# Sliding-window attention into a two-layer MLP: 96-row query and key loads, 544-column key blocks, a reordered opening and attention steps ahead of each group

## The chip, the cores and the metric

One core of one Trainium2 chip. The metric is device time in microseconds (us) of one execution, as the median of several. Engines are named TensorE (PE in the profile, PEld for its weight loads), VectorE (DVE), ScalarE (ACT), GpSimd (POOL) and SyncE (SP, which here only issues transfers).

## The reference

```python
# q, k, v: (8 batches, 8 heads, 576 tokens, 64), float32
scores = scale * q @ k^T;  masked to |i - j| <= 32;  softmax over j
x = (attn @ v) as (4608 tokens, 512)
h = x @ w_in            # (512, 2048)
g = max(0.01 * h, h)
out = g @ w_out         # (2048, 512)
```

The two products of the MLP are 589,824 of the 737,280 columns that TensorE streams in the kernel before. The attention is small for TensorE, but each of its 64 steps (a batch, half of its tokens, a pair of heads) passes through all four engines.

## The kernel before

A step scores the next pair and finishes the present one. `weighted` is the part that VectorE paces: one `s` buffer and one `x` buffer, a reciprocal (1.96 us in the profile before), a multiply (0.46 us).

```python
def score(i):            # five matmuls into ps, exp on ScalarE, mask multiply on GpSimd -> pr
    ...
def weighted(i):         # ones_bd x pr -> s (row sums), vbd x pr -> x
    ...
    nc.vector.reciprocal(r, s)
    nc.vector.tensor_mul(xT[:, p, t0:t0 + HALF], x, r)

def step():
    i = state["done"]; b, r = i // 8, i % 8
    step_transposes(...)             # next batch's q and k, a group at a time
    if i + 1 < NC: score(i + 1)
    weighted(i)
    if r in (0, 1): cast_qk(b + 1, r)          # GpSimd
    if r == 2: load_qks(b + 2)
    if 2 <= r < 6: cast_v(b + 1, r - 2)        # GpSimd
    if r == 6: load_vs(b + 2)
    state["done"] += 1
```

The queries and keys come in with 64 tokens of a head on 64 partitions, in pieces of 256 bytes. The MLP takes the tokens in groups of 256, then 512; each group is cut into chunks (a few h tiles, or one o tile), and a group's share of attention steps is spread over its chunks, each step BEHIND its chunk:

```python
groups = [(0, 256)] + [(256 + 512 * i, 512) for i in range(8)] + [(256 + 512 * 8, 256)]
need = [4 * -(-(t0 + n) // HALF) for t0, n in groups]   # steps that a group's tokens need
...
for ci, (kind, a, m) in enumerate(chunks):
    want = start + -(-(goal - start) * (ci + 1) // len(chunks))
    todo = want - state["done"]
    ...                                # the chunk's h tiles or its o tile
    for _ in range(todo):
        step()
```

The softmax here doesn't subtract the row's maximum and nothing guards it: scores larger than these inputs give would overflow.

## Time and profile before

| | before |
|---|---|
| median of the runs | 421.28 us (418.67 to 422.35) |
| profiled span | 421.2 us |
| mean granted TensorE clock | 0.974 |

The page's first part gives busy us, share of the span and instructions of each engine; in its second part each digit is the busy share (or granted clock) of a fortieth of the span, 10.5 us, in tenths.

```profile
PE 338.7 (80%) x2464; PEld 194.5 (46%) x2464; DVE 202.3 (48%) x204; ACT 164.5 (39%) x289; POOL 176.5 (42%) x220
...
PEclk9999999989999899989999999999899989989999
DMA  9999999445871937192450956396301100110111
```

The DMA engines are full (busy 90% or more) for the first seven slices. The clock dips six times, one slice each, to 0.8.

### The profile page before, as it was taken

The page shows a single profiled execution, that of the slowest core. Times are in us where ns is not written, and L with a number is a line of the kernel's source. Part 1 is how long each engine was busy: PE and PEld are TensorE (multiplying, and loading weights), DVE is VectorE, ACT ScalarE, POOL GpSimd, SP SyncE. Part 2 cuts the span into 40 slices and gives each one's busy share as a digit, 9 for nine tenths or more (in the row PEclk, how much of TensorE's full clock was granted, in tenths as well). Part 3 has the DMA queues.
Part 4 walks back from the last instruction along what each step waited for, and adds up shares of the span by engine and source line. Part 5 has one row for each costly group of instructions (what it writes and reads, how often), then busy time and mean ns, then how long its engine had stood idle before and what let it go on. Part 6 is the DMA issues. An engine that isn't in the chain of part 4 may idle for free.

```text
span 421.2 us, 6100 instructions
## 1 busy us (share of the span) xinstructions
PE 338.7 (80%) x2464; PEld 194.5 (46%) x2464; DVE 202.3 (48%) x204; ACT 164.5 (39%) x289; POOL 176.5 (42%) x220
## 2 busy tenths in 40 slices
PE   0231058766999799979999997999899799989996
PEld 0120046643555365545555554565455445534472
DVE  6112043866466457634445765568357735740111
ACT  1140033622752274237237525732473255116050
POOL 8992153746426443633216553654355413200000
PEclk9999999989999899989999999999899989989999
DMA  9999999445871937192450956396301100110111
GB/s 163 207 202 198 190 136 193 77 69 122 130 114 61 205 60 138 61 199 43 92 121 4 197 136 102 65 188 128 60 0 46 55 2 2 51 50 2 50 51 50
DMA packets 119835, 42.33 MB, mean 100 GB/s; under 512 B 112640, under 2 KB 114688, under 8 KB 119808
## 3 DMA queue, kind: packets, MB, share of 16 engines
q1 hardware_dynamic: 117056, 37.76, 50.7%
q0 software_dynamic: 2752, 4.20, 5.5%
q8 instruction: 19, 0.31, 0.3%
q14 instruction: 8, 0.07, 0.1%
HBM read 36.70 MB, written 9.44 MB: 110 GB/s over the span
## 4 chain that ended last, share of the span: by engine, by line
PE 73%; POOL 9%; DVE 7%; SPq 3%; issue 3%; ACT 3%; DMA 2%; POOLq 0%; DVEq 0%
PE mm L236 31%; PE mm L245 29%; DVE r L224 5%; PE s L217 3%; SPq L65 3%; PE tp L168 3%; PE x L217 3%; PE ps L197 3%; DMA kf<-in_k_dram 2%; POOL pr L205 2%; POOL mask L128 1%; POOL mask L124 1%; DVE xT L226 1%; ACT qT L174 1%; POOL w_in_bf L290 1%
## 5 line engine op out<-in xcount | busy, mean ns | idle before, releaser
L236 PE MATMUL mm<-xT,w_in_bf 128*128 128x512 bf16 (+1 forms) x640 | 142.3, 380 | 17.2 <-DVE xT L226 17.2
L224 DVE RECIPROCAL r<-s 128x288 f32<-128x288 f32 x64 | 125.2, 1957 | 58.0 <-PE s L217 56.6
L205 POOL TENSOR_TENSOR pr<-e,mask 128x576 bf16<-128x576 bf16 x64 | 81.4, 1272 | 169.2 <-ACT e L203 168.8
L245 PE MATMUL mm<-w_out_bf,gT 128*128 128x512 bf16 x576 | 130.7, 382 | 0.0
L240 ACT ACTIVATE gT<-mm 128x512 bf16<-128x512 f32 (+1 forms) x160 | 88.7, 554 | 94.0 <-PE mm L236 92.7
L236 PEld LDWEIGHTS <-w_in_bf 128*128 128x128 bf16 x640 | 64.0, 103 | 81.8 <-issue 30.0
L245 PEld LDWEIGHTS <-gT 128*128 128x128 bf16 x576 | 54.8, 99 | 62.1 <-issue 1.7
L250 DVE COPY o_sb<-mm 128x512 f32<-128x512 f32 x36 | 24.9, 691 | 70.8 <-PE mm L245 70.8
L174 ACT ACTIVATE qT<-tp 128x640 bf16<-128x640 bf16 (+1 forms) x32 | 20.7, 648 | 80.4 <-PE tp L168 80.4
L187 DVE COPY kbd<-tp 64x640 bf16<-64x640 bf16 (+1 forms) x32 | 14.8, 461 | 76.8 <-ACT kbd L185 76.7
L203 ACT ACTIVATE e<-ps 128x576 bf16<-128x576 f32 x64 | 41.2, 643 | 22.5 <-PE ps L197 22.4
L168 PE MATMUL tp<-ident,qb 128*128 128x128 bf16 x144 | 14.7, 235 | 35.7 <-POOL qb L147 31.9
L185 ACT ACTIVATE kbd<-tp 64x640 bf16<-64x640 bf16 (+1 forms) x32 | 20.5, 641 | 48.5 <-PE tp L168 48.5
L217 PE MATMUL s<-pr,ones_bd 128*128 128x128 bf16 (+1 forms) x320 | 27.7, 220 | 8.3 <-POOL pr L205 7.4
L226 DVE TENSOR_TENSOR xT<-x,r 128x288 bf16<-128x288 f32 x64 | 29.3, 458 | 6.7
L168 PEld LDWEIGHTS <-qb 128*128 128x128 bf16 x144 | 11.5, 105 | 42.0 <-POOL qb L147 32.3
L197 PE MATMUL ps<-qT,kbd 128*128 128x128 bf16 (+1 forms) x320 | 27.9, 220 | 1.2 <-ACT e L203 1.1
L217 PE MATMUL x<-pr,vbd 128*128 128x128 bf16 (+1 forms) x320 | 27.9, 220 | 0.1
L168 PE MATMUL tp<-ident,kb 128*128 128x128 bf16 x144 | 14.6, 234 | 16.0 <-ACT qT L174 8.3
L197 PEld LDWEIGHTS <-kbd 128*128 128x128 bf16 x320 | 22.6, 102 | 5.1 <-issue 2.3
L217 PEld LDWEIGHTS <-ones_bd 128*128 128x128 bf16 x320 | 20.0, 101 | 9.3 <-DVE r L224 5.0
L147 POOL CAST qb<-qf 128x1152 bf16<-128x1152 f32 x16 | 18.3, 1143 | 12.2 <-DMA qf<-in_q_dram 12.1
(25 smaller groups left out, 123.2 us busy)
## 6 DMA issues: line engine op xcount, KB each, us to landing
qf<-in_q_dram SPq DMA_DIRECT2D x32, 288.0 KB, 5.3
kf<-in_k_dram SPq DMA_DIRECT2D x32, 288.0 KB, 6.1
vf<-in_v_dram SPq DMA_DIRECT2D x16, 576.0 KB, 7.5
out_dram<-o_sb SPq DMA_DIRECT2D x36, 256.0 KB, 2.1
w_in_bf<-in_moe_w_in_dram POOLq DMA_DIRECT2D x8, 256.0 KB, 9.0
w_out_bf<-in_moe_w_out_dram POOLq DMA_DIRECT2D x4, 512.0 KB, 13.1
```

What stands on the lines that cost most here:

```text
L168: nc.tensor.transpose(tp[:, c - c0].rearrange("p s i -> p (s i)"), src[:, c, u].rearrange("p a d -> p (a d)"), ident,)
L174: nc.scalar.activation(out=qT[b][:, :, u, 64 * c0:64 * c1].rearrange("p s (c i) -> p c s i", i=64), in_=tp[:, 0:n], func=AF.Copy,)
L197: nc.tensor.matmul(ps[:, c0:c0 + n], kbd[b % 2][:, p, blk, :], qT[b][:, p // 2, p % 2, q0:q0 + n], start=True, stop=True,)
L203: nc.scalar.activation(out=e, in_=ps[:, 0:576], func=AF.Exp, scale=scale)
L205: nc.gpsimd.tensor_mul(pr, e, mask[hf])
L217: nc.tensor.matmul(dst[:, a:a + n], ones_bd if w is None else w[:, p, blk, :], pr[:, c0:c0 + n], start=(n_ == 0), stop=(n_ == len(WIN[hf]) ...
L224: nc.vector.reciprocal(r, s)
L226: nc.vector.tensor_mul(xT[:, p, t0:t0 + HALF], x, r)
L236: nc.tensor.matmul(h[:, 0:n], w_in_bf[:, c, ts(f, 128)], xT[:, c, ds(t0, n)], start=(c == 0), stop=(c == DMC - 1),)
L240: nc.scalar.activation(out=gT[g][:, f, 0:n], in_=h[:, 0:n], func=AF.Prelu, alpha=0.01)
L245: nc.tensor.matmul(o, gT[g][:, f, ts(j, 128)], w_out_bf[:, f, :], start=(f == 0), stop=(f == FFC - 1),)
L250: nc.vector.tensor_copy(out=o_sb, in_=o)
```

## The change

The intent: fewer, longer pieces in the loads; less to load before the first weights; no wait for xT at the start of a group. Its parts:

1. **Layout.** Each of 96 partitions holds six consecutive tokens (1536 bytes a piece). Transposes give the tokens in another order, put right while ScalarE and VectorE read PSUM. Key blocks are ordered so that 544 columns do for 576, and s takes two matmuls for five. The two masks are copied out of one window, which GpSimd builds with 4 select instructions in place of 40.
2. **Reordered opening.** Batch 0 goes pair by pair through cast, transpose, score and step; the weights are issued behind all four pairs; batch 1's loads are held behind the last weight by two tiny transfers; the h tiles of the first 512 tokens are computed before batch 1's attention begins. From here on the q and k loads of the batch after next stand behind a batch's seventh step, not its third.
3. **Attention ahead.** Steps are issued AHEAD of a chunk, by a rule that must have a group's steps done two chunks before the group starts.

```diff
-    t = fload.tile([128, 2, 2, NB, D], FP32, name=name)        # 64 rows, 256-byte pieces
+    qf[b] = fload.tile([96, NPAIR, 2, RUN * D], FP32, name="qf")  # RUN = 6 tokens a row
 ...
+                tok = tp.rearrange("p c i -> p i c")              # token order while PSUM is read
+                    nc.scalar.activation(out=qT[b][:, p].rearrange("p (i c) -> p i c", c=RUN), in_=tok, func=AF.Copy)
 ...
-        if r == 2:
-            load_qks(b + 2)
-        if r == 6:
-            load_vs(b + 2)
+            if r == 6 and b + 2 < B:
+                new_batch(b + 2); load_qk(b + 2, 0, 4); load_v(b + 2, 0, 4)
 ... opening
+    for p in range(NPAIR):
+        cast_qk(0, p, p + 1, nc.vector)
+        next(first); next(first)
+        cast_v(0, p)
+        if p == 0: score(0)
+        else: step()
+    for fq in range(4): load_w_in(512 * fq, 512 * fq + 512)
+    ...                                   # w_out; clears of kbd[1], vbd[1] on GpSimd
+    ...                                   # tiny transfers from w_out into qf[1], kf[1]; then batch 1's loads
+    step()
+    for f in range(FFC):
+        h_tile(0, 256, f)
+        if f % 4 == 3: step()
+    for f in range(FFC): h_tile(256, 256, f)
+    cast_qk(1, 0, 4); ...                 # casts of v
+    o_tile(0, 0); o_tile(0, 1)
+    step_transposes(16)
+    ...
 ... pacing
+    groups = [(512, 256)] + [(768 + 512 * i, 512) for i in range(7)] + [(768 + 512 * 7, 256)]
+    LEAD = 2
+    for ci, (_, kind, t0, n, a, m) in enumerate(chunks):
+        ahead = chunks[min(ci + LEAD, len(chunks) - 1)][0]
+        goal = max(ahead, base + -(-(NC - base) * (ci + 1) // span))
+        while state["done"] < min(goal, NC):
+            step()
+        ...                               # the chunk
```

## The prediction

> **What bounds the kernel now.** I read the page (shares, chain), then a table of stretches, then TensorE's waits, then the timeline of the opening and of one group of attention steps. TensorE is 80% busy and the chain is 73% TensorE, but the busy share hides two different halves. In the table of stretches (columns: stretch, length, busy time of PE, PEld, DVE, ACT, POOL, granted clock, DMA share, GB/s):
>
> ```profile
> 22.00:66.40 44.40, 12.48 (x104) 10.54 (x104) 11.77 (x13) 8.09 (x13) 22.39 (x28) 1.00 1.15 184
> ...
> 120.00:400.00 280.00, 261.92 (x1864) 142.35 (x1862) 148.34 (x150) 118.98 (x203) 108.17 (x108) 0.97 0.43 82
> ```
>
> Before 66 us TensorE is nearly idle while the DMA engines are full; after it TensorE sets the pace. The timeline shows what the opening waits for: the batch-1 key load, caught in a queue with all weights.
>
> ```profile
> 46.60 1.14 POOL L147 CAST qb<-qf 128x1152 bf16<-128x1152 f32 x1 [12.12 <-DMA qf<-in_q_dram]
> ...
> 54.94 1.15 POOL L147 CAST kb<-kf 128x1152 bf16<-128x1152 f32 x1 [7.20 <-DMA kf<-in_k_dram]
> ...
> 66.45 3.78 PE L236 MATMUL mm<-xT,w_in_bf 128*128 128x256 bf16 x17 [1.73 <-DVE xT L226]
> ```
>
> TensorE's waits from 66.4 us to the end, in us, times, longest:
>
> ```profile
> PE mm L236 <- DVE xT L226: 17.2, 8, 2.3
> PE tp L168 <- ACT qT L174: 5.4, 6, 1.0
> PE s L217 <- POOL pr L205: 2.9, 3, 1.0
> ```
>
> Each group of 512 tokens begins with an h tile that waits 2 us for the attention step just ahead of it: one reciprocal and one multiply on VectorE. The last thing to read is the pace of two attention steps with nothing between them:
>
> ```profile
> 79.97 0.42 PE L217 MATMUL s<-pr,ones_bd 128*128 128x128 bf16 x5
> ...
> 80.43 1.96 DVE L224 RECIPROCAL r<-s 128x288 f32<-128x288 f32 x1 [1.65 <-PE s L217]
> ...
> 82.58 0.41 PE L217 MATMUL s<-pr,ones_bd 128*128 128x128 bf16 x5 [1.00 <-POOL pr L205]
> ...
> 83.44 1.96 DVE L224 RECIPROCAL r<-s 128x288 f32<-128x288 f32 x1
> ```
>
> The s tile has one buffer, so the second step's s starts only after the first reciprocal: 2.6 us from s to s, of which TensorE works 0.95. A step that stands alone between two chunks of matmuls costs TensorE nothing extra; a step next to another costs it about 1.7 us.
>
> **Budget of now.** Sixteen 512-column matmuls start at 108.11 and the next instruction at 111.57: 3.46 us, 0.422 ns a column. All matmuls move 737,280 columns (589,824 in the two products, 3 x 64 x 576 attention, 288 x 128 transposes): 311 us. At 66.45 some 14,400 of these are done (6.1 us), so the opening loses 60.4. The last copy ends at 417.96 and the end is 421.2: with the copy, a tail of 3.9. The middle loses the rest, 46: waits of 28.5 (17.2 for xT), and half-speed clock windows of about 10 (granted clock 0.83 in 90 to 100 us, 0.96 in five of the seven 40 us stretches up to 400), 7 unnamed.
>
> [...] batch 0, loaded 64 partitions at a time, moves at 206 GB/s from 4 to 18 us. [...] the change takes q and k to 1536 bytes. [...]
>
> **The change part by part.**
> *Loads.* Packets of q and k fall from 73,728 to 12,288. After 90 us the DMA share is under two thirds and TensorE waits for a load-fed cast only once (2.7 us), so in the middle this is worth about 3 us. It counts in the opening alone.
> *544 columns.* 64 x 32 x 3 columns fewer: 731,136, or 308.5 us; minus 2.6. s takes 2 matmuls for 5. GpSimd's multiply falls from 1.27 to an estimated 1.20 us.
> *96-row transposes.* 384 x 96 columns, the same as now. ScalarE copies 576 columns twice a pair, about 0.65 us each as the 640/512 ones do (0.70/0.60); VectorE's two key copies replace one of 0.46 by two of perhaps 0.25. GpSimd casts 96 x 768 per pair, a third more elements: 64 x 0.77 against 32 x 1.145, plus 12 us, which the mask (11 us) pays. None of these is near a bound.
> *Opening.* GpSimd's order is the crux. It first clears vbd as 4608 elements (0.83 ns each from the two memset forms, 3.9 us), then builds the window, ready near 8 us. Then for each of four pairs: key cast 0.8, transposes 0.75, PSUM copy 0.75, two key copies 0.6, score 0.75, exp 0.65, multiply 1.3, and only then the next pair's key cast. That is 5.7 us a pair, so the weight loads, placed behind the fourth multiply, are issued near 34 us (19 now), with the DMA engines idle from about 18. Weights took 28 us from first issue (19.0) to the last landing (about 47); alone I keep 27: 61 us. Behind them GpSimd clears two more tiles (8 us), so the fifth multiply and with it the second h chunk start near 53; the h tiles of 512 tokens end near 73, two o tiles near 80. Batch 1 is loaded only after the weights: k lands near 75, v near 81, casts to 86. Eight transpose groups at 1.2 us run 80 to 89, the first score, exp and multiply bring steady work to 92 us. By then TensorE has done batch 0's attention, 16 transpose groups, 512 tokens of h and 256 of o: 72,500 columns, 30.6 us. The opening loses 61 us: as much as now.
> *Attention ahead.* The order of the changed kernel's TensorE queue shows the xT wait gone: o tiles of the last group stand between a group's last attention step and its first h tile. But the rule "be ahead two chunks before the group" makes steps come in bunches: two runs of six, three or so of three, some of two, and chunks of 64 matmuls with no step at all. I count 19 steps that stand right behind another (now 4 after the opening). 19 x 1.75 = 33 us; the runs of six also hold the next batch's q and k casts, 3.1 us of GpSimd per step for two steps: plus 5. Single-buffer transposes as now: 5. Clock windows at half speed after 7 to 8 such runs: 10. Together 53 against 46 now.
>
> Sum: 308.5 + 61 + 53 + 3.9 = 426.
>
> **Rivals.** (1) *The opening is much shorter*: if pairs pipeline at 4 us instead of 5.7 and the memsets are cheap, weights start near 25 us and steady work near 80: about 412, or 400 with the bunches milder than counted. For it: 15 us less of small-packet traffic ahead of the weights, and a plan that was clearly meant for this. Against it: GpSimd's multiply stands in its queue ahead of the next cast. (2) *The xT wait goes and the bunches are absorbed*: minus 17 and nothing back, about 390 to 400. Against it: one s buffer and 2.6 us a step, seen three times in the trace. (3) *The bunches cost more*: casts of a batch just loaded block GpSimd in the middle of a run, [...]the next chunk runs at half speed: 440. (4) *Strided PSUM reads slow ScalarE*: at double cost plus 40 us on an engine busy 164: it would stay below TensorE's total but lengthen every h chunk; about 435.
>
> **Range and chances.** The sum reproduces the kernel before only up to 7 us that I could not name, and the opening is a chain of some 25 links, each good to a tenth. That is 12 us either way around 426; against it, a reordering with such tuned constants was probably kept because it helped. I take 424, 399 to 441. Below 412.9 is faster by 2%: 0.28. Between: 0.38. Above 429.7: 0.34.
>
> **What would show it.** Right: weight loads issued after 30 us; a DMA gap in front of them; the first o tile after 70 us and steady work near 90; "s waits for reciprocal or multiply" as the largest wait of TensorE in the middle, 25 us or more, in two runs near the first two 512-token groups; no xT wait of note. Wrong: weights issued by 25 us; h tiles dense from 45 us; runs of six taking under 12 us; a middle (after steady work begins) losing under 35 us. ScalarE's copies at 1 us or more would be rival 4. What would make the total wrong most easily is the opening: every microsecond of the pair chain counts four times.

Its sum: 308.5 (columns) + 61 (opening) + 53 (middle) + 3.9 (tail) = 426. The 10 us of half-speed clock within the 53 are the author's estimate, carried over from the old trace (0.83 at 90 to 100 us, 0.96 in five later stretches).

## More of the kernel before

One more view is used later, the table of stretches for 31.3 us of the steady part, with the reciprocals (one for each attention step) that run in it, from the view of the r tile:

```profile
105.80:137.10 31.30, 30.51 (x246) 17.72 (x245) 19.20 (x19) 16.73 (x29) 15.12 (x15) 1.00 0.60 102
```

```profile
L224 DVE RECIPROCAL r<-s x7: 1947/1958/1958, 108.1 to 135.8; 128x288 f32<-128x288 f32 x7
```

TensorE is busy 30.5 of 31.3 us while seven steps pass. Where seven steps meet 30 us of matmul columns, they are hidden.

## The result, and the profile after

| | before | after |
|---|---|---|
| median of the runs of the same rounds | 420.45 us | 447.91 us (445.89 to 447.93) |
| ratio of fast runs | | 1.0641 [1.0581, 1.07] |
| profiled span | 421.2 us | 444.2 us |
| mean granted clock | 0.974 | 0.915 |

A ratio is the mean time of one kernel's fast runs over that of the other's fast runs of the same rounds, so it is not quite the ratio of the medians. Executions over 1.5% slower than the fastest of the same kernel are left out of the means. The result is correct and 6.4% slower, above the predicted range.

The page after, the lines that answer to those of before (a slice is now 11.1 us):

```profile
PE 351.4 (79%) x2432; PEld 201.8 (45%) x2432; DVE 220.6 (50%) x245; ACT 164.6 (37%) x301; POOL 188.4 (42%) x214
...
PEclk9999789969876999569999999997999899979999
DMA  7405979694650106901069029408900010100111
```

TensorE's busy time grew although it has fewer columns to stream: the clock dips deeply from slice 9 to 18 (to 0.5 to 0.8 in six of the ten), and matmuls at half speed are busy twice as long (back to back, a 128x512 matmul starts 0.43 us behind the one before it, 0.22 at full speed; from 94.3 us on, 21.1 us worth of columns fell into half-speed stretches and kept TensorE busy for 41.7 us). The DMA engines now have an empty slice from 22 to 33 us. TensorE's waits of the kernel after (us in all, times, longest):

```profile
PE s L220 <- DVE r L234: 18.9, 12, 2.2
PE s L220 <- POOL pr L212: 17.6, 9, 10.1
PE tp L166 <- DVE qb L146: 17.1, 3, 11.1
PE ps L202 <- DVE kbd L186: 7.2, 4, 1.8
...
PE mm L246 <- DVE xT L236: 1.8, 1, 1.8
```

The xT waits are gone (one of 1.8 us is left), and waits of s for the reciprocal and the multiply stand in their place; of these 36.5 us, 11.2 fall into the opening. The timeline of the opening after:

```profile
37.58 5.10 POOL L303 DMA_DIRECT2D w_in_bf<-in_moe_w_in_dram  x8
...
51.73 3.96 POOL L322 MEMSET vbd<- 128x4608 bf16 x1
...
56.91 0.40 PE L220 MATMUL s<-pr,ones_bd 128*128 128x288 bf16 x1 [10.10 <-POOL pr L212]
...
68.72 6.82 PE L246 MATMUL mm<-xT,w_in_bf 128*128 128x256 bf16 x61 [1.80 <-DVE xT L236]
...
75.37 7.07 PE L255 MATMUL mm<-w_out_bf,gT 128*128 128x512 bf16 x32
```

The weights are issued at 37.6 us (19.0 before), the fifth step waits 10.1 us for a multiply that stands behind two clears of 3.96 us, and dense work runs from 68.7 to 82.4 us. The first step of batch 1 follows at 94.3 us. Two moments in the runs of six steps that the lead makes:

```profile
125.66 1.96 DVE L234 RECIPROCAL r<-s 128x288 f32<-128x288 f32 x1
...
127.67 0.30 PE L220 MATMUL s<-pr,ones_bd 128*128 128x288 bf16 x1 [2.17 <-DVE r L234]
```

```profile
179.00 1.59 POOL L146 CAST qb<-qf 96x768 bf16<-96x768 f32 x2 [3.29 <-DMA qf<-in_q_dram]
...
179.87 0.66 PE L166 MATMUL tp<-ident,qb 96*128 96x96 bf16 x6 [2.84 <-POOL qb L146]
```

In the first, a step's s waits 2.17 us for the reciprocal of the step before it; in the second, the cast of a batch that has only just been loaded holds up the transposes inside the run.

**Where the time went.** A count that compares the kernels at equal work: add up all columns that TensorE has streamed at 0.4217 ns each (the prediction has 0.422), and call the clock time minus that sum the time lost so far. The marks are 30, 60 and 200 us worth of columns; the last column is the end of the span. No matmul records are missing from the two traces.

| lost, us, at | 30 us of columns | 60 | 200 | end |
|---|---|---|---|---|
| before | 75.8 | 77.1 | 92.1 | 110.3 |
| after | 61.2 | 84.5 | 117.9 | 135.9 |
| after minus before, since the last mark | -14.6 | +22.0 | +18.4 | -0.2 |

With 2.6 us fewer columns, the sum is 23.0 us, the difference of the spans. So the changed kernel is *ahead* by 14.6 us when it has done as much as the kernel before has by 106 us, and then gives back 40. The stretch from 30 to 60 us of columns, after, with its reciprocals:

```profile
91.20:144.50 53.30, 41.26 (x344) 28.08 (x342) 36.96 (x41) 21.25 (x42) 35.62 (x41) 0.78 0.52 114
```

```profile
L234 DVE RECIPROCAL r<-s x12: 1958/1958/1958, 94.9 to 138.4; 128x288 f32<-128x288 f32 x12
```

The same amount of matmul columns that took 31.3 us before takes 53.3, at a granted clock of 0.78, and twelve steps pass in it instead of seven. Whether that is a cause or a companion is for the experiments.

### The profile page after: what moved, and what is told of

The parts are those of the page before. It is cut to its first block, busy times and chain, and to the rows that moved or that the text cites. A ratio compares the mean times of both kernels' runs of the same rounds, so it can differ in the third digit from the quotient of the medians.

```text
span 444.2 us, 6092 instructions
## 1 busy us (share of the span) xinstructions
PE 351.4 (79%) x2432; PEld 201.8 (45%) x2432; DVE 220.6 (50%) x245; ACT 164.6 (37%) x301; POOL 188.4 (42%) x214
## 4 chain that ended last, share of the span: by engine, by line
PE 65%; DMA 12%; DVE 10%; POOL 5%; issue 3%; ACT 3%; SPq 2%; DVEq 0%; POOLq 0%; ACTq 0%
PE mm L255 29%; PE mm L246 25%; DVE r L234 6%; PE tp L166 3%; DMA w_out_bf<-in_moe_w_out_dram 3%; DMA kf<-in_k_dram 3%; DMA vf<-in_v_dram 3%; PE x L228 3%; PE ps L202 2%; POOL pr L212 2%; DMA w_in_bf<-in_moe_w_in_dram 2%; PE s L220 2%; SPq L73 1%; PE s L221 1%; POOL kb L146 1%
## 5 line engine op out<-in xcount | busy, mean ns | idle before, releaser
L212 POOL TENSOR_TENSOR pr<-e,mask 128x544 bf16<-128x544 bf16 x64 | 77.4, 1213 | 178.1 <-ACT e L208 172.6
L208 ACT ACTIVATE e<-ps 128x544 bf16<-128x544 f32 x64 | 39.8, 622 | 31.7 <-PE ps L202 28.9
L220 PE MATMUL s<-pr,ones_bd 128*128 128x288 bf16 x64 | 20.7, 323 | 36.5 <-DVE r L234 18.9
L186 DVE COPY kbd<-kT 64x576 bf16<-64x576 bf16 x64 | 28.5, 446 | 38.5 <-ACT kT L183 37.9
L174 ACT ACTIVATE qT<-tp 128x576 bf16<-128x576 bf16 x32 | 20.8, 649 | 63.1 <-PE tp L166 63.1
L154 POOL CAST vbd<-vf 64x576 bf16<-64x576 f32 x64 | 42.9, 670 | 2.4 <-DMA vf<-in_v_dram 0.5
L202 PE MATMUL ps<-qT,kbd 128*128 128x128 bf16 (+2 forms) x320 | 28.9, 227 | 9.0 <-DVE kbd L186 7.2
L228 PE MATMUL x<-pr,vbd 128*128 128x128 bf16 (+2 forms) x320 | 29.9, 232 | 1.3 <-DVE xT L236 0.8
L146 POOL CAST kb<-kf 96x768 bf16<-96x768 f32 x32 | 26.1, 841 | 6.3 <-DMA kf<-in_k_dram 6.2
L228 PEld LDWEIGHTS <-vbd 128*128 128x128 bf16 x320 | 24.0, 109 | 8.4 <-issue 4.8
L202 PEld LDWEIGHTS <-kbd 128*128 128x128 bf16 x320 | 20.5, 106 | 13.1 <-DVE kbd L186 8.0
## 6 DMA issues: line engine op xcount, KB each, us to landing
kf<-in_k_dram SPq DMA_DIRECT2D x14, 576.0 KB, 10.1
```

Of the source, the lines that this page charges most:

```text
L146: eng.tensor_copy(out=dst[:, p], in_=src[b][:, p].rearrange("p a (c d) -> p c a d", d=D),)
L154: nc.gpsimd.tensor_copy(out=vbd[b % 2][r, p, :, r], in_=vf[b][r, p])
L202: nc.tensor.matmul(ps[:, c0:c0 + n], kbd[b % 2][:, p, blk], qT[b][:, p, q0:q0 + n], start=True, stop=True,)
L208: nc.scalar.activation(out=e, in_=ps[:, 512 - HALF:512 - HALF + NCOL], func=AF.Exp, scale=scale,)
L212: nc.gpsimd.tensor_mul(pr, e, mask[hf])
L220: nc.tensor.matmul(s, ones_bd, pr[:, 0:HALF], start=True, stop=False, skip_group_check=True)
```

## The experiments

First theory, from the result: the bunching of steps costs more than predicted. Rival: the layout (casts, copies, PSUM reads) is what is slow. Four runs separate layout, opening and lead; each also ran beside the kernel before (421.25 us median in those rounds).

**e1, steps evenly spread ahead of chunks.** The changed kernel, with one edit:

```diff
-        ahead = chunks[min(ci + LEAD, len(chunks) - 1)][0]
-        goal = max(ahead, base + -(-(NC - base) * (ci + 1) // span))
-        while state["done"] < min(goal, NC):
+        want = start + -(-(goal - start) * (ci + 1) // len(chunks))   # per group, as before
+        while state["done"] < want:
             step()
         ...                               # the chunk
```

> The changed kernel, with one thing undone: the attention steps of a group are spread evenly, each ahead of its chunk, the last ahead of the group's last o tile, in place of bunches two chunks before the next group. Theory 'bunching' (steps that stand right behind one another run at VectorE's 2.6 us instead of TensorE's 0.95[...]): what is lost after 94 us falls from 67 us to about 35, so 412 to 418 us, granted clock back to 0.95 or more, the wait of s for the reciprocal below 8 us (18.9 now). Rival 'the opening or the new layout is what costs': stays within 2% of the changed kernel, 440 to 450 us.

Measured: 404.62 us (402.86 to 405.41), ratio 0.9618 [0.9574, 0.9661], clock 0.974 (0.915 in the changed kernel): faster still than the theory expected. Waits of s for the reciprocal fall from 18.9 to 3.5 us. The rule of the lead costs 43 us against an even lead.

**e2, the same steps evenly behind chunks**, as the kernel before has them.

> As e1, but each step stands behind its chunk, as in the kernel before, so that the last step of a group stands right ahead of the next group's first h tile. Theory 'bunching': 425 to 432 us, with the wait of h for xT back at 14 to 18 us in 7 or 8 pieces; the difference to e1 is what the lead is worth. Rival 'opening or layout': 440 to 450 us as the changed kernel.

Measured: 432.03 us (430.73 to 436.35), ratio 1.0293 [1.0228, 1.0359]. The xT wait is back in full:

```profile
PE mm L246 <- DVE xT L236: 20.4, 8, 2.9
```

So a lead is worth 27 us when it is even, and the change's rule turns this gain into a loss of 16.

**e3, the kernel before with the change's pacing loop alone.**

> The kernel before with the 'attention ahead' loop of the change and nothing else (old loads, 576 columns, old opening). Theory 'bunching': slower than before by 15 to 25 us, 436 to 446 us, granted clock near 0.92, no xT wait but 15 us or more of s waiting for the reciprocal or the multiply. Rival 'opening or layout': faster than before by the 17 us of xT waits, about 404 us.

Measured: 439.68 us (439.13 to 440.15; a fourth, slow execution took 445.85), ratio 1.0451 [1.0392, 1.0509]. No xT wait is left, and these two have come:

```profile
PE s L217 <- DVE r L224: 14.7, 13, 1.8
PE s L217 <- POOL pr L205: 12.4, 9, 3.8
```

The bunching is a cost of the rule, on the old layout too (+18.4 us).

**e4, the layout alone** (new loads, transposes, PSUM reads, masks and 544 columns; opening, later loads and pacing as before).

> The kernel before with only the new loads, transposes, PSUM reads and 544 columns; opening order and pace of steps as before. Both theories of the bunches say nothing here. Layout harmless: 415 to 421 us (2.6 us fewer columns, some DMA relief in the opening). Layout harmful (strided PSUM reads, two more VectorE copies a pair, more GpSimd cast time): 428 us or more.

Measured: 408.59 us (404.51 to 409.18), ratio 0.9697 [0.9638, 0.9756]. The rival is refuted: the layout gains 12.7 us, more than the 0 to 6 expected. Dense h tiles start at 48.14 us where they started at 66.45:

```profile
48.14 6.13 PE L245 MATMUL mm<-xT,w_in_bf 128*128 128x256 bf16 x29 [1.78 <-DVE xT L235]
```

What of this is the loads and what the shorter mask was not separated. In the kernel before, the first cast starts right behind the last select of the masks; in e4 it starts at 8.03 us, as soon as the queries have landed:

```profile
14.61 1.14 POOL L147 CAST qb<-qf 128x1152 bf16<-128x1152 f32 x1
```

That leaves a surprise: e2 and e4 differ in the opening (with the groups of tokens that go with it) and in the place of the later loads, and this, called the reordered opening below, costs 23.4 us. The next theory was late weights, with DMA engines idle from 20 us (share 0.00 to 0.01 from 20 to 37 us in the changed kernel).

**e5, e4 with the even lead.**

```diff
+            while state["done"] < want:
+                step()
             ...                           # the chunk
-            while state["done"] < want:
-                step()
```

> Kernel: the new loads, transposes, PSUM reads and 544 columns with the OLD opening, and the steps spread evenly but placed AHEAD of each chunk. Theory (the three parts add: layout -13, reordered opening +23, bunched lead +16, even lead against even lag -20 or more): the eight waits for xT of the layout-only run (20.6 us) go, little comes back, the median is 383 to 392 us, the waits for xT are under 5 us and the mean clock above 0.97. Rival A (the even lead helped only because the reordered opening left slack): 400 us or more, the wait for xT replaced by waits of the same size for the reciprocal or the multiply.

Measured: 383.16 us (381.82 to 383.33), ratio 0.9075 [0.9045, 0.9105], as expected and faster than both kernels.

**e6, e7, e8: repairs of the opening, on top of e1** (404.6 us), one after the other.

```diff
+        # e6: in the pair loop, w_in behind pair 0's casts, w_out behind pair 1's (not behind all four pairs)
-    # e7: as e6, without the two tiny transfers from w_out that hold batch 1's loads
-    nc.gpsimd.memset(kbd[1], 0.0); nc.gpsimd.memset(vbd[1], 0.0)
+    nc.vector.memset(kbd[1], 0.0); nc.vector.memset(vbd[1], 0.0)      # e8: as e7, with this
```

> Kernel: the changed kernel with the even lead (404.6 us), and w_in issued behind the first pair and w_out behind the second pair, instead of behind all four. Theory (the reordered opening loses its time because the weights are issued only at 37 us with the DMA engines idle from 18 us, so that everything behind them is late): w_in issued before 20 us, w_out landed near 45 us instead of 62, steady steps of batch 1 start 12 to 18 us earlier, median 387 to 394 us. Rival B (the pair chain and GpSimd's order, the two clears above all, set the opening, not the weights): 400 to 405 us. Rival C (the weights' transfers slow the first loads): slower than 405.

> Kernel: as e6, and without the two tiny transfers that hold the loads of batch 1 behind the last weight. Theory: batch 1 then lands beside the weights, GpSimd casts it as soon as its queue gets there, and the gap between the second o tile and batch 1's first step closes; 3 to 8 us under e6, DMA share above 1 from 20 to 50 us. Rival: the loads of batch 1 delay the weights as much as they gain, within 3 us of e6 or slower.

> Kernel: as e7, and the two clears of batch 1's tiles (two of 3.96 us on GpSimd) go to VectorE. Theory: the fifth multiply no longer waits behind them (10.1 us of TensorE waiting for it in the changed kernel), median 4 to 8 us under e7 (380 to 386). Rival: the weights set when the h tiles can go on, then within 2 us of e7.

Measured: e6 395.47 us (393.89 to 399.42), e7 395.18 us (394.69 to 396.08), e8 398.98 us (398.03 to 399.86). Late weights are 9 us of the opening's price, less than expected. The gate is worth nothing, a miss. Moving the clears made things worse, a miss too: they now stand in VectorE's queue (1.98 us each) ahead of a reciprocal and its xT multiply, and in that trace an h tile waits 5.9 us for xT. Twelve us to e5 remained.

**e9, the reciprocal replaced by a copy** (changed kernel; wrong result).

```diff
-        nc.vector.reciprocal(r, s)
+        nc.vector.tensor_copy(out=r, in_=s)
```

> Kernel: the changed kernel with the reciprocal (1.96 us) replaced by a plain copy of the same tile; wrong result on purpose (it multiplies by the sum). Theory (the pace of bunched steps is the one s tile held by VectorE's reciprocal): TensorE's waits of s for the reciprocal fall from 18.9 us to under 4, start to start of s in the bunches from 2.6 to 3.3 us to under 2.2, the half-speed stretches shrink with them, and the median falls from 448 to 415 to 428 us. Rival (GpSimd's casts and multiplies set the pace of the bunches): the waits for the multiply grow by what the others lose and the median stays above 438.

Measured: 430.75 us (429.3 to 433.01; a fourth, slow execution took 437.06), ratio 1.0245 [1.016, 1.033]. It lies between the two expectations. The copy takes 0.46 us for 1.96 and the waits for the reciprocal vanish, but 12 us come back as waits for the multiply, now 29.6 us for 17.6:

```profile
PE s L220 <- POOL pr L212: 29.6, 21, 9.9
```

VectorE (reciprocal 1.96 us, multiply 0.46) sets the pace of bunched steps, with GpSimd (multiply 1.2 us, and casts of 3.2 us in some steps) close behind it. Without the reciprocal's time 17 us come back of the 43 that the rule costs.

**e10, the query and key loads four steps earlier** (changed kernel: behind a batch's third step, as before, not behind the seventh).

> Kernel: the changed kernel with the query and key loads of the batch after next issued behind the third step of a batch, as before, instead of behind the seventh. Theory: in the second run of six, near 180 us, the two waits of TensorE for just-loaded casts (2.84 and 4.37 us) go and the median falls by 6 to 10 us, to 438 to 442. Rival: the casts stand behind multiplies in GpSimd's queue anyway and the bunch is VectorE's: within 3 us of 448.

Measured: 440.66 us (440.09 to 441.71), 7.3 us under the changed kernel, as expected. The transposes' waits in the second run of six (2.84 us in the lines above, and 4.37 us more for kb) are gone from TensorE's waits.

**e11, the kernel before with the even lead**: e5's edit on the old kernel and nothing else.

> Kernel: the kernel before with one edit, the evenly spread steps put AHEAD of each chunk instead of behind it. Theory (what the change wanted of the lead is the eight waits for xT, 17.2 us, and some half-speed clock; the bunching was not needed for it): 395 to 404 us, waits for xT under 5 us. With the layout-only pair (408.6 to 383.2, minus 25) it should be near 396. Rival: the lead pays only with the new layout, then above 412.

Measured: 396.3 us (394.16 to 396.63), ratio 0.9406 [0.9359, 0.9454]. Moving a loop ahead of a chunk, in the old kernel, is worth 25 us.

**e12, e5 with two repairs** (first group keeps its steps behind its chunks; v casts of batch 1 two steps later).

> Kernel: the old opening with the new layout and the even lead (383.2 us), where the first group keeps its steps behind its chunks and the first v casts of batch 1 stand two steps later, so that the multiply of the fifth step does not wait behind a v load. Theory: TensorE's wait of 7.5 us for that multiply goes, the first h tiles start near 46 us instead of near 57, median 373 to 380 us. Rival: h tiles so early wait for weights or for xT of the next group, then 381 or more.

Measured: 380.33 us (379.23 to 381.62), ratio 0.9039 [0.8993, 0.9085]. That is just above the expected 373 to 380. The trace still loses 15.5 us between 10 and 30 us of columns, where eight steps meet 20 us of columns.

**e13, the changed kernel with its opening undone**, the direct test of whether the parts add.

> Kernel: the changed kernel with its reordered opening undone (the old opening order, from the layout-only kernel) and its own attention-ahead loop kept. Theory (the parts add): 447.9 minus 23.4, or 408.6 plus 15.9: 421 to 428 us, so about the time of the kernel before. Rival A (the opening's price comes only with even pacing): 440 or more. Rival B (the bunches cost only because the opening left the steps late): 414 or less.

Measured: 434.69 us (433.55 to 436.17), ratio 1.031 [1.0275, 1.0345]. It fits none of the three: the parts do not add. (The later loads, which e13 puts back as well, are worth 7.3 us under this rule by e10, so the opening proper costs about 6 here.) With it the table of medians is complete:

| pacing | old kernel | new layout, old opening | new layout, reordered opening |
|---|---|---|---|
| even, behind chunks | 421.3 (before) | 408.6 (e4) | 432.0 (e2) |
| even, ahead of chunks | 396.3 (e11) | 383.2 (e5) | 404.6 (e1) |
| the change's rule | 439.7 (e3) | 434.7 (e13) | 447.9 (after) |

Down the columns the rule costs 16 to 26 us against even steps behind chunks, and 43 to 52 against even steps ahead. Along the rows the layout gains 13, 13 and 5; the reordered opening, with its later loads, costs 23, 21 and 13. With even steps the later loads were not tried alone; TensorE's waits for casts of q and k after 150 us are none in e2 and 2.6 us in e1.

**e14, the block of eight transpose groups spread between h tiles** (on e7).

```diff
-    for f in range(FFC): h_tile(256, 256, f)
-    cast_qk(1, 0, 4); ...
+    for p in range(NPAIR): cast_qk(1, p, p + 1)
+    ...
+    for f in range(FFC):
+        h_tile(256, 256, f)
+        if f % 2 == 1 and f >= 5: step_transposes(8 + (f - 3) // 2)
```

> Kernel: as e7 (395.2 us), but batch 1's casts are issued before the second set of h tiles and the eight transpose groups of batch 1 are put between those h tiles, one behind every second tile, instead of in one block behind two o tiles. Theory (the block of 9.4 us, of which TensorE works 4, and the half-speed clock behind it, are most of the remaining 12 us against 383): 385 to 390 us, no half-speed slice near 80 to 90 us. Rival (the rest of the opening, the serial pair chain of 7.4 us a pair, sets it): within 3 us of 395.

Measured: 395.45 us (392.56 to 395.89), so no gain on e7. The block is gone and the first step of batch 1 starts at 81.3 us instead of near 86, but the gain is taken away at once, in part by batch 2's casts waiting for batch 2's loads (TensorE waits 7.0 us for these casts up to 150 us, 3.5 in e7; the rest is not named):

```profile
89.87 1.59 POOL L146 CAST kb<-kf 96x768 bf16<-96x768 f32 x2 [2.98 <-DMA kf<-in_k_dram]
```

This result called for the count at equal work, the table of lost time above. The reordered opening loses no more than the old one by 30 us of columns; e1 and e5 stand at 62.6 and 62.1 us lost there. By 60 us of columns they stand at 85.9 and 63.3. The lines for that stretch, e1's and then e5's:

```profile
92.60:145.90 53.30, 41.04 (x340) 27.40 (x343) 36.16 (x40) 21.32 (x42) 34.74 (x40) 0.84 0.51 115
92.10:123.30 31.20, 30.46 (x237) 17.31 (x236) 20.77 (x25) 16.79 (x29) 17.82 (x22) 1.00 0.41 101
```

```profile
L233 DVE RECIPROCAL r<-s x7: 1957/1958/1960, 90.3 to 117.7; 128x288 f32<-128x288 f32 x7
```

By 60 us of columns both orders have done 20 steps. The old opening has 13 of them behind it at the 30 us mark; the reordered one has 8, and crowds 12 into the second 30 us. (Of e5's seven reciprocals above, the first starts before the mark.) It spent the dense matmuls of 512 tokens before batch 1's attention could begin, and put off five steps. Call this the **debt theory**: those matmuls would have hidden the steps. The same count over all 19 traces agrees with it: the second 30 us of columns take 31 to 32 us where six or seven steps start in them (six kernels), 42 to 44 with eight or nine (four), 51 to 58 with ten or twelve (nine, all with the reordered opening). The rival is that casts or loads of batches 1 and 2 are late whatever the order.

**e15, e16, e17: smaller groups.** Nothing of opening, loads or casts is changed; only the grouping, so that at most four steps fall due in 256 tokens (eight in the first 256 before).

```diff
-    groups = [(512, 256)] + [(768 + 512 * i, 512) for i in range(7)] + [(768 + 512 * 7, 256)]
+    groups = [(512 + 256 * i, 256) for i in range(6)] + [(2048 + 512 * i, 512) for i in range(5)]
     # e15: on e1;  e16: on e7;  e17: on e12, from token 0
```

> Kernel: the changed kernel with the even lead (404.6 us), and the tokens 512 to 2048 taken in groups of 256 instead of 512, so that at most four attention steps fall due per 256 tokens (with the old grouping eight fall due within the first 256). Nothing of the opening, the loads or the casts is changed. Theory (debt of attention steps): the 53 us for the second 30 us of columns become 36 to 42, 8 steps or fewer in that stretch, and the median falls to 388 to 395 us. Rival (casts and loads of batches 1 and 2 are late, whatever the grouping): within 4 us of 404.6.

> Kernel: as e7 (weights issued early, no gate; 395.2 us), with the same groups of 256 for the tokens 512 to 2048. Theory: the same 10 to 16 us as in e15, so 379 to 385 us, about the time of the old opening with the even lead (383.2): then late weights and the debt together are the opening's whole price. Rival: within 4 us of 395.

> Kernel: as e12 (380.3 us, old opening), with groups of 256 for the tokens up to 2048. Theory: e12 loses nothing to debt in its second 30 us of columns (31.3 us for them) but 11 us between 10 and 30 us of columns, where eight steps fall due in the first 256 tokens; small groups take part of this: 373 to 379 us. Rival: matmuls of 256 columns cost ScalarE and TensorE what they gain: 380 or more.

Measured: e15 393.72 us (393.44 to 394.35), e16 385.07 us (384.5 to 385.42), e17 370.23 us (368.61 to 371.08; ratio 0.8783 [0.8741, 0.8825]). The median falls by 10.9, 10.1 and 10.1 us. e15's stretch of the second 30 us of columns and its reciprocals:

```profile
92.50:134.30 41.80, 36.07 (x303) 24.28 (x304) 27.93 (x31) 18.03 (x38) 23.30 (x27) 0.88 0.68 154
```

```profile
L234 DVE RECIPROCAL r<-s x9: 1946/1958/1959, 95.8 to 132.7; 128x288 f32<-128x288 f32 x9
```

Nine steps for twelve, 41.8 us for 53.3. The debt theory's rival, within 4 us, is refuted, and two gains add: early weights 9 us (e1 to e7), due dates of steps 10 us (e7 to e16), which reaches 385.1 where the old opening with the even lead has 383.2. But this is not yet the opening's price taken apart, because small groups give the old opening the same 10 us (e12 to e17). At equal grouping the reordered opening stays behind: e16 is 15 us slower than e17, of which 3 are e12's repairs (383.2 to 380.3). The second 30 us of columns, e16's and then e17's:

```profile
83.60:125.50 41.90, 36.17 (x303) 24.35 (x304) 27.91 (x31) 18.01 (x38) 23.28 (x27) 0.88 0.66 148
77.90:108.70 30.80, 30.69 (x281) 21.90 (x281) 23.27 (x25) 16.42 (x38) 16.85 (x20) 1.00 0.58 147
```

Most of the gap, 11 us, lies in this stretch, where nine steps start in e16 and seven in e17: the debt is smaller, not gone. About 6 us (53.6 lost against 47.9 at the 30 us mark) lie before it. The serial chain of pairs, 6 to 7.5 us a pair between the multiplies at 15.5, 21.4, 28.9 and 36.4 us, may hold those; neither part was tried by itself.

e17 beats both kernels, by 12% against the kernel before.

## Why the prediction was right or wrong

**The direction's mechanism was right.** The budget held the xT waits to go and bunched steps to cost more, for a net loss (426 in the sum); e2 and e1 show the first and e3 the second. Of what it said would show it right: the weights were issued at 37.6 us (near 34 predicted), the DMA engines had a gap before, two o tiles ended at 82.4 us (80), steady work began at 94.3 us (92). Waits of s for the reciprocal and the multiply sum to 25.3 us after 94.3 us (17.8 and 7.5; 25 or more predicted), and xT is down to 1.8.

**The failed step is the middle term: 53 us predicted, 68.3 measured.** The whole sum of the prediction was 308.5 + 61 + 53 + 3.9; from the trace it is 308.3 + 63.6 + 68.3 + 3.8 = 444. The stalls that it named were not too small: TensorE's waits after 94.2 us sum to 37.8 us, against 43. Those for the reciprocal and the multiply are 19, as many as the steps it counted behind another, but of 1.33 us each and not 1.75 (25.3 us for 33); waits for casts of q and k are 7.2 (5), for the single transpose buffer 4.4 (5). Two other terms were mis-sized. Half-speed clock was put at 10 us and cost about 19 (the extra time of the columns streamed at half speed; 10 in the old middle). And 12 us had no term: the 7 us that could not be named in the old budget were left out of the new one. They are not idle time. TensorE is idle for 38 us of the middle, as the waits say, and busy for 30 us more than its columns need, 19 of them for half speed (before: idle 27, busy 19 more, 10 of them for half speed); what makes up the rest was not found.

The prediction carried 10 over from the old kernel to a kernel with more stalls: 75.8 us of the changed trace run at half speed, against 23.7 us before (in the middles 57.6 and 20.5). In the clock records of the two traces the half-speed stretches last 3.4, 6.8, 10.2, 13.7 and 20.5 us, all multiples of 3.4 us (but for those that the end cuts short). In the 3.4 us before each of the changed kernel's seven falls from 87 us on, TensorE was busy for 1.0 to 1.4 us and its longest pause was 2.2 us; before the old middle's six falls it was busy for 1.1 to 1.4 us and paused for 2.3 us at most, and for 1.5 us before the one that makes the 0.83 at 90 to 100 us. So these falls came behind stretches of short waits, and short waits are what bunched steps make. Stalls of TensorE and clock could not be budgeted apart here: e9 took the reciprocal's waits away and half-speed time fell with them, from 75.8 to 47.1 us.

**"The opening loses 61 us: as much as now" was right as a number and misleading as a comparison.** It set 61 us at 92 us, with 30.6 us of columns done, against 60.4 us at 66 us, with 6.1 done. At equal work the changed opening is 14.6 us *better* off. What it owes lies behind it, in steps put off, and there the prediction had no term: it counted which steps stand right behind one another (19 times 1.75 us) and not how many steps fall due per column of dense work. e1, in which the rule of the lead is gone, still needs as long for that stretch (53.3 us); e15 shortens it to 41.8 by grouping alone. e13's failure to add can be read the same way, though no run tested this reading: opening and rule share the stretch from 30 to 60 us of columns. The rule adds 11.7 us there on the old opening (43.5 us in e13 against 31.8 in e4) and 0.6 on the reordered one (53.3 against 52.7 in e2). Some matmul records are missing from the traces of e1 to e4 and e13 to e17 (6 to 8 us of 308, under 1 us in 30 if evenly spread), so those stretches are good to about 1 us.

**Layout.** The prediction gave the loads about 3 us in the middle and said that they count in the opening alone. That is confirmed as to place, with all of e4's gain there at the 30 us mark (61.6 us lost, against 75.8), but the sum gave this gain no term of its own, because the reordered opening was priced as a whole. VectorE's two key copies took 0.45 us each, not the 0.25 estimated.

**The rivals.** (1) A short opening: the layout does that (e4), the reordering does not. (2) Bunches absorbed: no, but an *even* lead is what it described, and e11 shows it at 396.3 us, within its 390 to 400. (3) Bunches that cost more, with casts of a batch just loaded in the middle of a run and a next chunk at half speed, at 440: this is what came, with 8 us more; e10 measures its cast part as 7.3 us. (4) Strided PSUM reads that slow ScalarE: refuted, 0.649 us for 576 columns, as estimated (before, 0.701 for 640 and 0.595 for 512).

**The shading.** 426 became 424 because "a reordering with such tuned constants was probably kept because it helped". No view of the profile supported that, and the chances of faster, 0.28, were fed by it as well.

## What to carry to other kernels

Put fine-grained work evenly AHEAD of the chunks that need it; a deadline rule that makes it come in bunches can cost more than the wait it removes (here 17 us of waits went and the rule still left the kernel 16 to 26 us slower than even steps behind the chunks). When work is reordered, compare two kernels at equal work done and not at a named moment, and ask how much dense work is left for every step that is still due: spending it early is a debt. A transfer or clear is worth moving only after asking in which queue it will then stand.

## What the runs measured of the hardware

- Loads: with the layout alone (q and k on 96 rows together with v on 64), 240 GB/s moved from 4 to 16 us, against 206 from 4 to 18 us before: 1.17 times. The pieces of q and k also grew from 256 to 1536 bytes, and no run separates the two.
- VectorE beside GpSimd: VectorE's cast of the identity took 4.28 us in the changed kernel, where GpSimd's clear of 3.94 us ran beside it, and 0.57 us before. In e4, where VectorE itself does that clear later, the cast took 0.41 us; no run changed that alone.
- Clears: a 128 by 4608 bf16 tile took 1.98 us on VectorE, written as 2304 uint32 elements a row, and 3.96 us on GpSimd, where it stayed bf16; no run separates the engine from the type.
- Reciprocal: 1.96 us for 128 by 288 float32 from PSUM, against 0.46 us for a copy of the same tile (e9).
- Clock: the falls to half speed (from 87 us on in the changed kernel, in the middle of the old) came after stretches of 3.4 us with TensorE busy for 1.0 to 1.4 us and no pause over 2.3 us. The changed kernel ran 75.8 us at half speed, and 22.6 us when only the spread of the steps was changed (e1).
